# A hand-written operation list for the first three batches, put in another order

## The chip, the cores and the metric

The kernel runs on one core of one Trainium2 chip. The metric is the device time of one execution in microseconds, as the median of several runs. The times in the profile are counted from the start of its span.

## What is computed

Cosformer linear attention is followed by an MLP mixer. There are 8 batches, 8 heads, 576 positions and a head dimension of 64. Inputs and output are float32.

```python
theta = pi/2 * arange(S) / S                       # S = 576
phi(x) = concat([relu(x)*cos(theta), relu(x)*sin(theta)], -1)     # 64 -> 128 features
kv  = phi(k)^T @ v         # per batch and head: 128 x 64
z   = sum over positions of phi(k)
x   = (phi(q) @ kv) / (phi(q) @ z + 1e-6)          # heads side by side: 576 x 512 per batch
h   = relu(x^T @ w_tok1) @ w_tok2                  # mixes positions, 576 -> 256 -> 576
u   = x + h^T
out = u + relu(u @ w_ch1) @ w_ch2                  # mixes channels, 512 -> 1536 -> 512
```

## The kernel before

The 576 positions of a batch are laid on 128 partitions as four full column groups and a half one (j = 0 to 4, `J` = 4, `JA` = 5). Two batches share one tile for their half groups, `u_tail`, which is treated at the very end as if it were more batches. Raw q and k have two SBUF buffers each (even and odd batches), raw v has one. PSUM is split into two pools: `psA` with 2 buffers of two banks and `psM` with 4 buffers of one bank. A buffer is taken again only after the engine that evacuates it is done.

For a batch the steps are these; the names are the words of the operation list. `feat.b.t.j.g.f.E` computes one feature block (`f` 0 cosine, 1 sine) of q or k on engine E (L331 on ScalarE, L333 on VectorE). `cast` turns v into bfloat16 (L265). `turn` transposes q features on TensorE (L346) and `turno` evacuates them (L265); from batch 2 on `turnx` does it with a DMA on SyncE's queue (L355). `kvm` and `kvo` are kv (L362) and its copy. `num` (L391, L395) multiplies by kv, and `numo` divides on VectorE (L408, L414); `numf` and `numfo` do it for both halves of the heads (L410 to L414). `mix` is the first token product (L434), `mixo` its relu. `ux` and `ut` make the transposed u for batch 0 directly (L445, L451), `uto` copies it. `um` and `uo` make u in its normal layout (L461, L466), `tm` and `to` the tail (L489, L495). For batch 1 `ubc` casts u and `utr`, `utro` transpose it on TensorE (L481); later ones use the DMA transpose `utx` (L473). `up` is the first channel product (L513; for batch 0 the first four are split in halves of the contraction, `up.0.2.0.2` and `up.0.2.2.4`), `upo` and `upo2` its relu. `dnw` and `dnj` are the second channel product (L525), and `o` adds and stores (L537, L540).

Loads of q, k and v are `ld.b.t.g` on SyncE's queue, each of two DMAs (L144). Weights are loaded, with a conversion from float32 to bfloat16, on GpSimd's queue: `wt1` (L233), `wt2` (L239), `wu.a.n` (n of the 12 column blocks of `w_ch1` from block a, L244) and `wd.a.n` (row blocks of `w_ch2`, L249). `w2a` lays `w_tok2` out anew (L265). A last word such as `q12` in `wu.2.2.q12`, or `k02` or `wd3`, is a gate: the DMA isn't issued until that transfer has landed (q of batch 1, all heads; k of batch 0; the `wd` from block 3). `warm.0.tr.0.0.25` gives TensorE 25 transposes of zeros (L312), `warm.0.b1...` full matmuls of zeros (L322).

**What sets the order.** For batches 0, 1 and 2, and the features of batch 3, the order is the string `PLAN` (lines 17 to 57). Its words are read one after another and each issues its instructions at once (L633 to L639). Each engine takes its instructions strictly in that order, so an instruction that waits holds up all that stand behind it on the same engine, DMA issues on the SyncE and GpSimd queues among them. An engine doesn't depend on the others except by data, by buffers that come free, and by gates. The first four loads (q, k, and v in two halves of the heads, of batch 0) are issued ahead of the list (L157 to L162). 20 matmuls of zeros (L193) come first on TensorE. From batch 2's channel product on, the function `channel` runs with a table of hooks (L641 to L677); it begins at the first instruction of L590.

Of the kernel before, what the change touches and what calls it, by code (L numbers as in the profile page):

```python
# [14 lines left out]
WARM = 20  # L15
FIRST = "S"
PLAN = """
mkid feat.0.q.2.2.0.D feat.0.q.0.2.1.D feat.0.q.1.2.0.A wt1.k02 feat.0.q.3.2.0.A feat.0.q.0.2.0.D
feat.0.q.4.2.0.D feat.0.k.4.2.0.D wt2 feat.0.k.0.2.0.A feat.0.q.1.2.1.D warm.0.tr.0.0.25 turn.0.0.0 wu.4.4.k02
feat.0.k.4.2.1.D turn.0.0.1 feat.0.k.2.2.1.A feat.0.k.0.2.1.D feat.0.k.1.2.1.A feat.0.q.4.2.1.D  # L20
feat.0.k.3.2.0.A warm.0.tr.2.0.19 turn.0.2.0 turno.0.2.0.A turno.0.0.0.A cast.0.3.2.0.D feat.0.q.3.2.1.D
feat.0.k.1.2.0.D feat.0.q.2.2.1.D warm.0.tr.1.0.26 turn.0.1.0 turno.0.1.0.A cast.0.0.3.0.P feat.0.k.3.2.1.D
feat.0.k.2.2.0.D kvm.0.0 kvo.0.0.A cast.0.0.3.1.P cast.0.3.2.1.P kvm.0.1 num.0.0.0 turno.0.0.1.D numo.0.0.0
w2a.0.A warm.0.b1.0.0.4 mix.0.0.0 num.0.1.0 w2a.1.P turn.0.1.1 num.0.2.0 ld.1.q.2.v01 kvo.0.1.D num.0.0.1
turn.0.2.1 mix.0.1.0 wu.2.2.wt2 numo.0.1.0 turno.0.1.1.A mix.0.2.0 num.0.1.1 turno.0.2.1.A num.0.2.1 mix.0.3.0
numo.0.0.1 numo.0.2.0 mix.0.4.0 mixo.0.0.A wu.0.2.v01 wu.8.4 mix.0.0.1 feat.1.q.0.2.0.A numo.0.1.1 mix.0.1.1
ux.0.0 feat.1.q.0.2.1.A mix.0.2.1 mix.0.3.1 ux.0.3 numo.0.2.1 mix.0.4.1 ux.0.1 ut.0.1 mixo.0.1.D ut.0.0
uto.0.0.A ut.0.3 um.0.0 feat.1.q.4.2.0.A feat.1.q.3.2.0.D feat.1.q.1.2.1.A uto.0.1.D up.0.2.0.2 up.0.3.0.2
feat.1.q.1.2.0.D ux.0.2 ut.0.2 turn.1.0.1 uo.0.0 feat.1.q.2.2.1.A ld.1.k.2.q12 uto.0.3.D feat.1.q.3.2.1.D
uto.0.2.A up.0.0.0.2 ld.1.v.0.wu2 turn.1.0.0 feat.1.q.4.2.1.D turno.1.0.0.D feat.1.q.2.2.0.A turno.1.0.1.D  # L30
up.0.2.2.4 ld.1.v.1 turn.1.1.1 wd.9.3.k12 cast.1.4.1.0.P up.0.1.0.2 turn.1.2.0 turno.1.2.0.D turn.1.2.1 wd.0.3
up.0.0.2.4 wd.6.3.v10 up.0.1.2.4 upo2.0.0.D turno.1.1.1.A up.0.7 upo.0.7.D feat.1.k.2.2.1.A turn.1.1.0
turno.1.1.0.A feat.1.k.0.2.1.D up.0.3.2.4 up.0.10 up.0.8 tm.0 upo.0.8.A feat.1.k.4.2.0.A up.0.6 wd.3.3.v10
feat.1.k.3.2.0.D turno.1.2.1.D to.0 upo2.0.1.A ld.2.k.2.v11 up.0.11 feat.1.k.1.2.0.D upo.0.10.A
feat.1.k.0.2.0.A cast.1.0.4.0.D feat.1.k.2.2.0.D feat.1.k.1.2.1.A feat.1.k.4.2.1.D feat.1.k.3.2.1.D um.0.1
uo.0.1 cast.1.4.1.1.A upo.0.11.D up.0.4 up.0.9 upo.0.6.A upo.0.9.A kvm.1.0 ld.2.q.2.wd6 kvo.1.0.D
cast.1.0.4.1.P kvm.1.1 kvo.1.1.D upo.0.4.A ld.2.v.2.wd0 ld.3.k.2.k22 num.1.1.0 numo.1.1.0 up.0.5 upo.0.5.A
num.1.1.1 numo.1.1.1 num.1.0.0 dnw.0.0 num.1.0.1 dnw.0.1 numo.1.0.0 feat.2.k.0.2.0.A numo.1.0.1 num.1.2.1
feat.2.k.2.2.1.A dnw.0.2 feat.2.k.4.2.0.A feat.2.k.3.2.0.A feat.2.q.3.2.1.A numo.1.2.1 mix.1.0.2 ld.3.q.2.q22
mix.1.1.2 mix.1.2.2 mix.1.3.2 dnw.0.3 num.1.2.0 dnw.0.4 numo.1.2.0 feat.2.k.2.2.0.D mix.1.4.2 mixo.1.2.D.1  # L40
mixo.1.2.D.0 feat.2.q.1.2.1.A feat.2.k.4.2.1.D feat.2.q.3.2.0.A feat.2.k.3.2.1.D dnw.0.5 dnw.0.6
feat.2.q.4.2.1.D feat.2.k.1.2.1.A feat.2.q.0.2.0.D um.1.1 uo.1.1 ubc.1.1 feat.2.k.0.2.1.A dnw.0.7 um.1.0
feat.2.q.0.2.1.A tm.1 feat.2.k.1.2.0.D uo.1.0 feat.2.q.2.2.1.D cast.2.4.1.2.A dnw.0.8 feat.2.q.1.2.0.A
turnx.2.0.2 dnw.0.9 dnw.0.10 feat.2.q.4.2.0.D to.1 cast.2.0.1.2.P utr.1.1 utro.1.1.A cast.2.1.1.2.P dnw.0.11
feat.2.q.2.2.0.D turnx.2.2.2 cast.2.3.1.2.D ubc.1.0 utr.1.0 utro.1.0.A turnx.2.4.1 o.0.2 o.0.0 cast.2.2.1.2.P
o.0.3 kvm.2.2 feat.3.k.4.2.1.A feat.3.k.2.2.0.D up.1.2 upo.1.2.A up.1.3 upo.1.3.D up.1.9 up.1.8
feat.3.k.1.2.1.A o.0.1 up.1.0 upo.1.9.A feat.3.k.0.2.1.D kvo.2.2.A numf.2.1 numfo.2.1 numf.2.0 numfo.2.0
feat.3.k.4.2.0.A up.1.7 tb.1 upo.1.7.A up.1.4 upo.1.4.A numf.2.2 numfo.2.2 upo.1.0.A feat.3.q.1.2.0.A numf.2.3
up.1.6 up.1.1 mix.2.0.2 numfo.2.3 numf.2.4 numfo.2.4 feat.3.k.0.2.0.D upo.1.6.A feat.3.q.1.2.1.A mix.2.1.2
mix.2.2.2 mix.2.3.2 feat.3.q.4.2.1.A feat.3.q.0.2.1.A feat.3.k.2.2.1.D feat.3.q.0.2.0.A mix.2.4.2 mixo.2.2.A  # L50
ld.3.v.2.wd3 up.1.10 upo.1.10.D turnx.3.0.2 feat.3.q.4.2.0.A turnx.3.4.1 feat.3.q.3.2.0.A up.1.5 upo.1.1.A
upo.1.8.A feat.3.k.3.2.1.D um.2.1 uo.2.1 ubc.2.1 upo.1.5.A um.2.0 uo.2.0 up.1.11 cast.3.0.1.2.D upo.1.11.A
dnj.1.3.0 utx.2.1 dnj.1.2.0 dnj.1.1.0 feat.3.k.3.2.0.A dnj.1.2.1 cast.3.2.1.2.D feat.3.q.3.2.1.A ubc.2.0
utx.2.0 dnj.1.0.0 feat.3.q.2.2.0.D feat.3.q.2.2.1.A turnx.3.2.2 ld.4.k.2 ld.4.q.2 o.1.2 dnj.1.1.1
cast.3.3.1.2.D cast.3.1.1.2.D cast.3.4.1.2.D ld.4.v.2.k42 dnj.1.0.1 o.1.0 dnj.1.3.1 o.1.3 feat.3.k.1.2.0.A tm.2
to.2 o.1.1
"""

@with_exitstack
# [650 lines left out]
```

## Time and profile before

| what | value |
|---|---|
| median of 5 runs | 276.68 us (275.57 to 277.37) |
| the profiled execution | 276.62 us, its span 274.9 us |
| TensorE (PE) busy | 263.1 us, 96% of the span |
| VectorE (DVE) busy | 171.3 us, 62% |
| ScalarE (ACT) busy | 114.9 us, 42% |
| GpSimd (POOL) busy | 48.5 us, 18% |
| DMA | 53.37 MB, mean 194 GB/s; SyncE's queue 66.7% of the 16 engines' span, the software queue of GpSimd 9.2% |
| first instruction of L590 | 91.31 us |

The page gives busy time by engine, then the span in 40 slices of 6.9 us, in tenths. A busy TensorE is not necessarily one with useful work, since the fillers count too. The timeline of an engine gives start, length, line and tiles of each group of instructions, and in brackets how long the engine was idle ahead of it and what ended that.

### The profile page before, as it was taken

The numbers are of one execution on the slowest core, as the hardware profiler recorded it, in microseconds if no ns is written. First come the engines' busy times: TensorE is split into PE (matmuls) and PEld (weight loads), VectorE is DVE, ScalarE is ACT, GpSimd is POOL, SyncE is SP. The second block draws the span as 40 slices with busy tenths as digits, with TensorE's granted clock in tenths as the row PEclk, the third lists the DMA queues.
The fourth block names the chain that finished last, engine by engine and source line by source line (L and its number), as shares of the span: only waits on it lengthen the run. The fifth ranks groups of instructions, "written<-read, shape, count | busy, mean of one in ns | idle before, by whom it ended". The sixth has DMA issues, their size and how long they took to land.

```text
span 274.9 us, 4808 instructions
## 1 busy us (share of the span) xinstructions
PE 263.1 (96%) x1901; PEld 137.0 (50%) x1920; DVE 171.3 (62%) x341; ACT 114.9 (42%) x181; POOL 48.5 (18%) x67
## 2 busy tenths in 40 slices
PE   6779999999999999999999999999999999999994
PEld 2567646445444554455445544554455444444443
DVE  6588789498773476947683869486738634323322
ACT  2555673377781339133913392339233201301300
POOL 2282060052030032600150017001100120000000
PEclk9999999999999999999999999999999999999999
DMA  6999999999999999998999958920990052003012
GB/s 205 313 189 244 326 178 228 348 356 206 220 271 168 357 376 362 219 223 277 334 176 249 338 177 154 192 95 2 193 230 2 0 132 118 0 31 122 2 59 95
DMA packets 79079, 53.37 MB, mean 194 GB/s; under 512 B 47824, under 2 KB 76496, under 8 KB 79056
## 3 DMA queue, kind: packets, MB, share of 16 engines
q1 hardware_dynamic: 74512, 48.77, 66.7%
q0 software_dynamic: 4144, 3.77, 9.2%
q10 hardware_dynamic: 400, 0.52, 0.5%
q8 instruction: 15, 0.25, 0.4%
q14 instruction: 8, 0.07, 0.1%
HBM read 35.85 MB, written 9.44 MB: 165 GB/s over the span
## 4 chain that ended last, share of the span: by engine, by line
PE 72%; DMA 2%; DVE 1%; issue 0%
PE c_ps L590 26%; PE o_ps L607 25%; PE b L434 4%; PE u L461 4%; PE o L525 4%; PE nf L391 3%; PE kv L362 3%; DMA qpT<-qp 2%; PE c L513 1%; PE o_ps L599 1%; PE ut L489 1%; DVE x L414 1%; DVE den L411 0%; DVE u_tail L601 0%; DVE den L410 0%
## 5 line engine op out<-in xcount | busy, mean ns | idle before, releaser
L269 ACT ACTIVATE h<-c_ps 128x512 bf16<-128x512 f32 x52 | 31.0, 597 | 108.5 <-PE c_ps L590 64.3
L607 PE MATMUL o_ps<-wc,h 128*128 128x512 bf16 x317 | 71.5, 379 | 0.4
L590 PE MATMUL c_ps<-uT,wc 128*128 128x512 bf16 x288 | 70.4, 379 | 0.0
L607 PEld LDWEIGHTS <-h 128*128 128x128 bf16 x324 | 31.7, 98 | 38.2
L590 PEld LDWEIGHTS <-wc 128*128 128x128 bf16 x336 | 30.8, 98 | 32.6
L271 DVE TENSOR_SCALAR h<-c_ps 128x512 bf16<-128x512 f32 x32 | 22.0, 688 | 28.4 <-PE c_ps L590 28.4
L265 POOL CAST ub<-u 128x1024 bf16<-128x1024 f32 x14 | 15.1, 1076 | 127.5 <-DVE u L466 83.8
L610 DVE TENSOR_TENSOR u<-o_ps,u 128x512 f32<-128x512 f32 x24 | 16.5, 688 | 18.5 <-PE o_ps L607 18.5
L331 ACT ACTIVATE qp<-qt,cos_t 128x512 bf16<-128x512 f32 x31 | 21.9, 713 | 4.1 <-DMA qt<-in_q_dram 4.1
L265 POOL CAST vbf<-vt 128x512 bf16<-128x512 f32 (+3 forms) x28 | 19.7, 740 | 20.0 <-DMA vt<-in_v_dram 19.8
L513 PE MATMUL c<-uT,wc 128*128 128x512 bf16 x96 | 23.1, 379 | 0.1
L525 PE MATMUL o<-wc,h 128*128 128x512 bf16 x93 | 22.0, 379 | 0.4 <-DMA wc<-in_moe_w_ch_dram 0.2
L331 ACT ACTIVATE qp<-qt,sin_t 128x512 bf16<-128x512 f32 x31 | 21.5, 711 | 1.5 <-DMA qt<-in_q_dram 1.5
L414 DVE TENSOR_TENSOR x<-nf,den 128x512 bf16<-128x512 f32 x30 | 20.7, 691 | 1.0
L466 DVE TENSOR_TENSOR u<-u,x 128x1024 f32<-128x1024 f32 x16 | 19.4, 1218 | 1.8 <-PE u L461 1.8
L434 PE MATMUL b<-x,w 128*128 128x512 bf16 (+1 forms) x84 | 20.0, 353 | 0.4
L391 PEld LDWEIGHTS <-qpT 128*128 128x128 bf16 x320 | 14.9, 98 | 9.1 <-DMA qpT<-qp 1.2
L333 DVE TENSOR_SCALAR kp<-kt,cos_t 128x512 bf16<-128x512 f32 x30 | 17.1, 571 | 2.8 <-DMA kt<-in_k_dram 2.8
L410 DVE TENSOR_SCALAR den<-nf 128x8 f32<-128x8 f32 x30 | 5.0, 165 | 18.8 <-PE nf L391 18.8
L333 DVE TENSOR_SCALAR kp<-kt,sin_t 128x512 bf16<-128x512 f32 x31 | 16.6, 545 | 0.0
L461 PE MATMUL u<-B,w 128*128 128x512 bf16 x64 | 16.3, 379 | 0.0
L525 PEld LDWEIGHTS <-h 128*128 128x128 bf16 x96 | 9.0, 97 | 10.5 <-issue 0.5
(94 smaller groups left out, 255.5 us busy)
## 6 DMA issues: line engine op xcount, KB each, us to landing
out_dram<-u SPq DMA_DIRECT2D x32, 256.0 KB, 2.6
qt<-in_q_dram SPq DMA_DIRECT2D x8, 640.0 KB, 8.0
kt<-in_k_dram SPq DMA_DIRECT2D x8, 640.0 KB, 8.2
qt<-in_q_dram SPq DMA_DIRECT2D x8, 512.0 KB, 6.9
kt<-in_k_dram SPq DMA_DIRECT2D x8, 512.0 KB, 6.8
vt<-in_v_dram SPq DMA_DIRECT2D x6, 640.0 KB, 9.4
vt<-in_v_dram SPq DMA_DIRECT2D x6, 512.0 KB, 8.4
wc<-in_moe_w_ch_dram POOLq DMA_DIRECT2D x4, 384.0 KB, 8.5
```

Of the source, the lines that this page charges most:

```text
L265: (nc.scalar.copy if eng == "A" else ENG[eng].tensor_copy)(dst, src)
L269: nc.scalar.activation(dst, src, AF.Relu)
L331: nc.scalar.activation(dst, src, AF.Relu, scale=tab)
L333: ENG[eng].tensor_scalar(dst, src, scalar1=tab, scalar2=0.0, op0=ALU.mult, op1=ALU.max)
L391: nc.tensor.matmul(nm[:, hh * (D + 1):(hh + 1) * (D + 1)], self.qpT[:, j * H + h, :], self.kv[:, h, :D + 1], start=(not eps or hh == 0), s ...
L414: nc.vector.tensor_mul(dst, nmv[:, :, :, :D], den_b)
L434: nc.tensor.matmul(b1[:, mi], w1[:, col(self.c, j), mi * P:(mi + 1) * P], self.x[:, j, cs], start=(j == 0 and (g == 2 or mi == 0)), stop=( ...
L461: nc.tensor.matmul(ps[:, jj], w2[:, ki, 1 + 2 * g + jj, :], self.B1[:, ki, :], start=(ki == 0), stop=(ki == NT - 1))
L513: nc.tensor.matmul(ps, wc1[:, ki, mi * P:(mi + 1) * P], self.uT[:, :, ki, :], start=(ki == 0), stop=(ki == NCC - 1))
L525: nc.tensor.matmul(self.ps["o", j], self.h1[:, ki, j * P:(j + 1) * P], wc2[:, ki, :], start=(ki == 0), stop=(ki == NCH - 1))
L590: nc.tensor.matmul(c_ps, wc1[:, ki, mi * P:(mi + 1) * P], uT[:, :, ki, :], start=(ki == 0), stop=(ki == NCC - 1))
L607: nc.tensor.matmul(o_ps, h1[:, ki, j * P:(j + 1) * P], wc2[:, ki, :], start=(ki == 0), stop=(ki == NCH - 1))
```

## The change

Only the string `PLAN` differs. The two lists have the same useful operations. What is moved, taken from another engine or gated in another way, in the order of the list:

- batch 0: VectorE's first word is a k feature (it was a q feature), five q features come first on ScalarE; the transposes are in another order, with 43 + 7 + 45 fillers in place of 25 + 19 + 26, and the four full matmuls of zeros are gone;
- the first cast of v on GpSimd stands ahead of `wt1` and `wt2`, which lose their gate on k; one cast goes from GpSimd to ScalarE; `ld.1.q.2` loses its gate on v and stands near the front; `wu.4.4` goes from first to last among the `wu`;
- batch 0's transposed q are all ahead of kv; heads' half 1 is done before half 0 in kv, `num` and `mix`;
- k of batch 1 is gated on `wu8` instead of q of batch 1, the two halves of v of batch 1 on `wu4` and on nothing;
- `up.0` takes the blocks in another order (9 and 11 first); the `wd` come in the order 0, 3, 6, 9 instead of 9, 0, 6, 3;
- batch 2: q is loaded first, then k and v; `turnx.2.2.2` and `turnx.2.0.2` stand ahead of the loads of batch 3; other engines for many features, casts and evacuations.

The core of the diff:

```diff
-mkid feat.0.q.2.2.0.D feat.0.q.0.2.1.D feat.0.q.1.2.0.A wt1.k02 feat.0.q.3.2.0.A feat.0.q.0.2.0.D
-feat.0.q.4.2.0.D feat.0.k.4.2.0.D wt2 feat.0.k.0.2.0.A feat.0.q.1.2.1.D warm.0.tr.0.0.25 turn.0.0.0 wu.4.4.k02
-feat.0.k.4.2.1.D turn.0.0.1 feat.0.k.2.2.1.A feat.0.k.0.2.1.D feat.0.k.1.2.1.A feat.0.q.4.2.1.D
-feat.0.k.3.2.0.A warm.0.tr.2.0.19 turn.0.2.0 turno.0.2.0.A turno.0.0.0.A cast.0.3.2.0.D feat.0.q.3.2.1.D
-feat.0.k.1.2.0.D feat.0.q.2.2.1.D warm.0.tr.1.0.26 turn.0.1.0 turno.0.1.0.A cast.0.0.3.0.P feat.0.k.3.2.1.D
-feat.0.k.2.2.0.D kvm.0.0 kvo.0.0.A cast.0.0.3.1.P cast.0.3.2.1.P kvm.0.1 num.0.0.0 turno.0.0.1.D numo.0.0.0
-w2a.0.A warm.0.b1.0.0.4 mix.0.0.0 num.0.1.0 w2a.1.P turn.0.1.1 num.0.2.0 ld.1.q.2.v01 kvo.0.1.D num.0.0.1
-turn.0.2.1 mix.0.1.0 wu.2.2.wt2 numo.0.1.0 turno.0.1.1.A mix.0.2.0 num.0.1.1 turno.0.2.1.A num.0.2.1 mix.0.3.0
-numo.0.0.1 numo.0.2.0 mix.0.4.0 mixo.0.0.A wu.0.2.v01 wu.8.4 mix.0.0.1 feat.1.q.0.2.0.A numo.0.1.1 mix.0.1.1
...
-uto.0.2.A up.0.0.0.2 ld.1.v.0.wu2 turn.1.0.0 feat.1.q.4.2.1.D turno.1.0.0.D feat.1.q.2.2.0.A turno.1.0.1.D
-up.0.2.2.4 ld.1.v.1 turn.1.1.1 wd.9.3.k12 cast.1.4.1.0.P up.0.1.0.2 turn.1.2.0 turno.1.2.0.D turn.1.2.1 wd.0.3
...
-cast.1.0.4.1.P kvm.1.1 kvo.1.1.D upo.0.4.A ld.2.v.2.wd0 ld.3.k.2.k22 num.1.1.0 numo.1.1.0 up.0.5 upo.0.5.A
...
+feat.0.k.4.2.0.D feat.0.q.0.2.0.A feat.0.q.2.2.1.A feat.0.q.3.2.1.A feat.0.q.4.2.1.D feat.0.q.3.2.0.A
+feat.0.q.2.2.0.A mkid ld.1.q.2 warm.0.tr.1.1.43 turn.0.1.1 feat.0.k.3.2.0.A feat.0.k.4.2.1.D turn.0.1.0
+feat.0.q.1.2.1.D feat.0.q.4.2.0.A feat.0.q.1.2.0.A feat.0.k.2.2.0.D feat.0.k.1.2.1.D cast.0.0.3.0.P
+warm.0.tr.2.1.7 turn.0.2.1 turno.0.2.1.A feat.0.k.0.2.1.D cast.0.3.2.0.D feat.0.k.1.2.0.D turno.0.1.0.A
+feat.0.q.0.2.1.D warm.0.tr.0.0.45 turn.0.0.0 feat.0.k.0.2.0.D turn.0.2.0 turno.0.2.0.D feat.0.k.3.2.1.A
+feat.0.k.2.2.1.A cast.0.0.3.1.A turn.0.0.1 wt1 turno.0.1.1.D wt2 cast.0.3.2.1.P kvm.0.1 kvo.0.1.D turno.0.0.1.A
+turno.0.0.0.A kvm.0.0 kvo.0.0.A num.0.0.1 numo.0.0.1 feat.1.q.1.2.1.A num.0.2.1 numo.0.2.1 num.0.0.0 numo.0.0.0
+num.0.1.1 numo.0.1.1 mix.0.0.1 num.0.1.0 wu.2.2.q12 numo.0.1.0 wu.0.2.v00 num.0.2.0 mix.0.1.1 ux.0.3 mix.0.2.1
+mix.0.3.1 mix.0.0.0 mix.0.1.0 numo.0.2.0 mix.0.2.0 feat.1.q.3.2.0.A feat.1.q.3.2.1.D mix.0.3.0 mix.0.4.0
+feat.1.q.1.2.0.A mix.0.4.1 mixo.0.1.D wu.8.4 feat.1.q.0.2.1.A w2a.1.A feat.1.q.2.2.1.D ux.0.1 feat.1.q.4.2.1.A
+mixo.0.0.A feat.1.q.2.2.0.D w2a.0.P ut.0.3 ux.0.0 uto.0.3.D ut.0.1 uto.0.1.D tm.0 ut.0.0 um.0.1 ux.0.2 ut.0.2
+feat.1.q.0.2.0.D turn.1.0.1 uto.0.2.A to.0 turn.1.1.0 uto.0.0.D up.0.9 upo.0.9.A up.0.11 upo.0.11.A wu.4.4.q12
+turno.1.0.1.D uo.0.1 ld.1.k.2.wu8 feat.1.k.1.2.1.A um.0.0 feat.1.k.4.2.0.A feat.1.k.3.2.0.A feat.1.q.4.2.0.D
+uo.0.0 ld.1.v.1.wu4 up.0.2.0.2 up.0.3.0.2 up.0.2.2.4 turno.1.1.0.D turn.1.1.1 feat.1.k.0.2.1.D ld.1.v.0 up.0.6
+feat.1.k.4.2.1.D up.0.4 feat.1.k.2.2.0.D up.0.0.0.2 wd.0.3.k12 wd.3.3 up.0.1.0.2 turno.1.1.1.D feat.1.k.1.2.0.A
+feat.1.k.2.2.1.D up.0.0.2.4 up.0.1.2.4 upo.0.6.D turn.1.2.1 turno.1.2.1.A upo.0.4.D up.0.3.2.4 upo2.0.0.A
+up.0.10 up.0.7 upo.0.10.A wd.6.3 feat.1.k.3.2.1.D cast.1.0.4.0.D cast.1.4.1.0.D turn.1.2.0 turno.1.2.0.D
...
+kvo.1.0.D wd.9.3.v11 cast.1.0.4.1.P cast.1.4.1.1.P kvm.1.1 kvo.1.1.D dnw.0.0 num.1.2.1 numo.1.2.1 ld.2.q.2.wd3
+feat.2.q.0.2.0.A num.1.0.0 numo.1.0.0 dnw.0.1 num.1.0.1 numo.1.0.1 dnw.0.2 ld.2.k.2.wd0 feat.2.q.3.2.1.A
...
+feat.2.q.2.2.0.D ld.2.v.2 feat.2.q.4.2.1.D feat.2.k.1.2.1.A feat.2.q.3.2.0.D feat.2.q.0.2.1.D turnx.2.2.2
+uo.1.1 ubc.1.1 feat.2.k.0.2.0.A um.1.0 turnx.2.0.2 uo.1.0 dnw.0.6 feat.2.k.3.2.1.D feat.2.k.2.2.0.D
...
+feat.2.k.4.2.1.A utr.1.1 utro.1.1.D utr.1.0 utro.1.0.D cast.2.3.1.2.D ld.3.q.2.q22 cast.2.2.1.2.D
...
+cast.2.0.1.2.P kvm.2.2 kvo.2.2.A turnx.2.4.1 ld.3.k.2.wd6 o.0.3 up.1.0 upo.1.0.A up.1.9 numf.2.3 numfo.2.3
+up.1.4 upo.1.9.A numf.2.1 up.1.2 numfo.2.1 upo.1.4.A o.0.1 up.1.5 numf.2.0 upo.1.5.A upo.1.2.A numfo.2.0
+feat.3.q.3.2.0.A feat.3.q.1.2.0.A feat.3.q.2.2.0.D ld.3.v.2.v22 cast.3.4.1.2.P up.1.10 up.1.3 numf.2.2
...
```

## The prediction

> **What bounds the kernel now.** I read the page's slices first. After the first slice TensorE is busy to the end, and so is DMA up to slice 25:
>
> ```profile
> PE   6779999999999999999999999999999999999994
> ...
> DMA  6999999999999999998999958920990052003012
> ```
>
> So the kernel is TensorE's own work plus whatever time TensorE does no useful work. The change adds no useful matmul and removes none, and from slot 0 of the first `channel` call (91.3 us) on the program text is the same. The question is therefore at what time TensorE gets there. Next I read TensorE's timeline from 9 to 21 us (start, length, line; in brackets the wait before it):
>
> ```profile
> 9.16 1.56 PE L312 MATMUL tr<-ident,zero 128*128 128x128 bf16 x25
> 10.55 0.39 PE L346 MATMUL tr<-ident,qp 128*128 128x128 bf16 x4
> 12.43 0.83 PE L346 MATMUL tr<-ident,qp 128*128 128x128 bf16 x12 [1.49 <-DVE qp L333]
> ...
> 17.56 0.62 PE L346 MATMUL tr<-ident,qp 128*128 128x128 bf16 x8 [1.56 <-DVE qp L333]
> ...
> 21.21 0.38 PE L434 MATMUL b<-x,w 128*128 128x256 bf16 x2
> ```
>
> L193, L312 and L322 multiply zeros, so they are filler. TensorE waits for features. From 21 to 91 us it is dense, with a few holes. I add up the start-to-start excess of each matmul over its usual spacing (512 columns 0.216 us, 128 columns 0.056, 65 columns 0.033): the holes are 0.15 and 0.28 at 43 us, 0.37 at 50.6, 0.15 at 57.5, 0.47 at 63.3, 0.48 at 71.1 and 0.31 at 73.9, together **2.2 us**. The last two wait for transposed q (timeline, 69 to 75 us):
>
> ```profile
> 71.37 0.68 PE L391 MATMUL nf<-kv,qpT 128*128 128x65 bf16 x16 [0.32 <-DMA qpT<-qp]
> ```
>
> The features are late because VectorE is slowed. Its timeline from 11 us, and GpSimd's:
>
> ```profile
> 12.99 0.48 DVE L333 TENSOR_SCALAR qp<-qt,sin_t 128x512 bf16<-128x512 f32 x1
> 13.39 0.42 DVE L265 CAST vbf<-vt 128x512 bf16<-128x512 f32 x1
> 13.72 1.17 DVE L333 TENSOR_SCALAR qp<-qt,sin_t 128x512 bf16<-128x512 f32 x1
> 14.81 1.72 DVE L333 TENSOR_SCALAR kp<-kt,cos_t 128x512 bf16<-128x512 f32 x1
> ```
> ```profile
> 12.00 1.91 POOL L233 DMA_DIRECT2D w<-in_moe_w_tok_dram  x2 [9.98 <-DMA kt<-in_k_dram]
> 13.91 0.73 POOL L239 DMA_DIRECT2D w2r<-in_moe_w_tok_dram  x1
> 14.63 0.79 POOL L244 DMA_DIRECT2D wc<-in_moe_w_ch_dram  x1
> 15.39 2.58 POOL L265 CAST vbf<-vt 128x768 bf16<-128x768 f32 x3
> ```
>
> A VectorE feature takes 0.40 us (start to start), but the four from 13.72 take 4.45 us instead of 1.6, while GpSimd issues `w2r` and `wc` and casts. The issue of `wt1` from 12.00 slowed nothing up to 13.72.
>
> **The start, worked out.** k of batch 0 is there at 11.40 (VectorE's first kp) and q at 6.93. Both stay, since their loads are not touched.
>
> *Features.* New: VectorE's first instruction needs k, so it idles to 11.40, while ScalarE does five q features at 0.615 each from 6.94, to 10.1. VectorE then has 10 features and one cast (10 x 0.40 + 0.33 = 4.3 us), the same number as before from that time on. GpSimd's cast now stands before the weights. It waits for the first half of v (its last packet ends 1.35 us before it counts as landed, as with k; that gives 12.8), then 0.86, `wt1` 1.91, `w2r` 0.73, second cast to 17.2. I charge VectorE 0.8 for the first cast, nothing for `wt1`, 0.5 for `w2r`: it ends at 11.4 + 4.3 + 1.3 = 17.0, with the last q feature at 16.6. Before, it ended at 18.57. Bounds: nothing charged (15.7), and the 2.87 that before lost (18.6).
>
> *TensorE.* Filler 25 -> 43 (43 x 0.056 = 2.4) runs to 11.55; the first two groups of transposes are ready then. 7 and 45 fillers end at 15.55, still ahead of the features, so the 25 added fillers cost nothing; if the features came before, up to 1 us. `turn.0.0.0` 16.6, `turn.0.0.1` ends 17.7, both kv products end 19.2. ScalarE evacuates 17.9 to 19.8 (two 128x1024, 0.95 each) and then kv (0.38) at 20.2. The first normalisation on VectorE starts at 19.7 instead of 20.22, and the chain is four long (0.90) and two short (0.55) ones = 4.7, to 24.4 (before: 25.7, with a kv cast and a wait inside). `num.0.1.0` waits for that chain to free PSUM (0.9 us). One q feature, then `mixo.0.1.D` at 25.1 to 25.8, and the token product `ut` starts at 25.85. Before it started at 26.33, with one `ux` more done (4 x 0.056 = 0.22). **Lead 0.26, say 0.3 us.** With the bounds of VectorE: +1.1 and -1.3.
>
> *The weights.* `wt1`/`wt2` are issued 1.8 us later (13.8 against 12.0) and share with q of batch 1, which is no longer held back until v lands (14.53). `wt1` took 4.0 us to land on the page; with the sharing about 18.9, needed at 21.0. `wt2` about 20.3, needed by the `w2a` copies at 22. q lands at about 20.7 instead of 25.9, which fills the thin DMA stretch at 13 to 17 us; nothing needs it so early, so that is worth nothing by itself.
>
> The skill speaks on two points. In the trace VectorE lost 2.87 us beside GpSimd. The Trainium skill, "SBUF — State Buffer", section "SBUF: two separate sides", says that a two-port VectorE operation and a GpSimd one exclude each other for a whole instruction, and that weight DMAs issued from GpSimd then wait for descriptors. By it `wt1` would be stopped by VectorE's features until 17 and land after 21, a loss of 1 to 2 us; the row speaks against that part, as `wt1` was issued in 1.91 us under five back-to-back VectorE operations (12.00 to 13.91). And TensorE runs transposes alone from 8.94 to 18.0 with a granted clock of 1.00, while "TensorE: Matmul & The Clock Gate", section "Part 4: PE-mode transpose", says that these don't count as activity. By that rule the longer filler would let the clock fall; by the row it stays.
>
> **The middle.** Order in GpSimd: q lands, `wu.2`, `wu.0`, `wu.8` issued 20.7 to 23.0 (0.76 each), `w2a.0` 1.4, then `wu.4`. k of batch 1 now waits for `wu.8` instead of q. The software queue moved about 380 KB/us of f32 at 24 to 29 us (its packets), so 2.1 MB from 21.8 land at 27.7. k is issued then, 1.9 us later than before:
>
> ```profile
> 25.89 1.98 SPq L144 DMA_DIRECT2D kt<-in_k_dram  x2
> ...
> 37.73 1.30 SPq L144 DMA_DIRECT2D kt<-in_k_dram  x2
> ...
> 51.48 2.38 SPq L144 DMA_DIRECT2D kt<-in_k_dram  x2
> ```
>
> Before, k took from 25.89 to 34.65 (ScalarE's wait), 8.76 us, beside 3.6 us of weights still moving; now 2.4 us are left (`wu.4`), so about 7.6: 35.3. What is queued behind: on ScalarE and VectorE the k features stand ahead of `turno.1.1.1.D` and `upo.0.6.D`, which free PSUM for `up.0.10` (TensorE gets there at 38.7) and `up.0.7` (39.55). From landing to the first is 3 x 0.40 + 0.6 = 1.8, to the second 2.9. So k may land as late as **36.6** without a wait; 1.3 us to spare, cost nothing. kv of batch 1 (42.8) needs the last k feature, at 41.7.
>
> From 40 us on q, k, v of batch 2 are loaded one after the other behind `wd.3`, without batch 3 between them, and the DMA transposes of j 0 to 3 stand ahead of batch 3's loads. The waits for qpT (0.48 + 0.31) go, and `wd` comes in the order of use (the 0.37 goes). What is late next: the casts of v of batch 2 stand on VectorE behind five k features and two copies, done at about 62.6 where kv wants it at 62.1 (0.5, as the 0.47 before), and `up.1.4` needs the bank that `o.0.3` frees after `to.1`, 65.8 against 65.45 plus a start (0.45 new). The 0.58 of the small ones I keep. So 2.2 becomes 0.58 + 0.5 + 0.45 = 1.5: **0.7 us gained**. Below 64 us batch 3 has time: last v lands at about 79, uT of batch 2 at 88.5, wanted at 90.3.
>
> **Sum.** The profiled execution took 276.62 (span 274.85 and 1.77 around it), 0.06 below the median 276.68. 276.62 - 0.3 - 0.7 = **275.6 us**.
>
> **Rivals.**
> - *Gains eaten at the port.* VectorE loses the whole 2.87 as before. Then the start is 1.3 behind, and with 0.7 from the middle the time is 277.2. For: GpSimd is busy in the same window. Against: only two casts, not three, and no `wc` issue there.
> - *Slower: k of batch 1 too late.* `wu.8` holds it, and it passes 36.6, whereupon VectorE and ScalarE stand in their k features and TensorE stops at `up.0.10`/`up.0.7`; each us later costs one us. For: the k load of 37.73, issued while all four `wd` were queued, landed only at 51.48, 13.7 us. Issued at 27.7 that would be 41.4, a loss of 4.8, 280.4; halfway (10.6 us, 38.3) it costs 1.7, 277.3. Against: only one weight transfer is queued behind it here, not four.
> - *Nothing moves.* The lead is not there and the waits that go are replaced by others of the same size, as TensorE was dense before as well: 276.6.
>
> **How the numbers follow.** Forecast 0.50, port 0.20, k late 0.18, nothing 0.12. About 0.3% (0.83 us) can be told from no change: faster is below 275.85. Of the forecast 0.40 is below it, 0.10 not. Port: 0.13 same, 0.07 slower; k late: 0.18 slower; nothing: same. Faster 0.40, same 0.35, slower 0.25. The forecast's own range is 274.6 to 276.4; over all cases 274.2 (VectorE charged nothing, 0.8 less, and some of the kept holes gone) to 278.6 (k late by 3 us).
>
> **What would show it.** VectorE's last batch-0 k feature ends near 17.0; `ut` starts near 25.9; ScalarE's first batch-1 kp near 35.3 with no TensorE wait at 38 to 40; no wait for qpT at L391; the first L590 matmul at about 90.3 instead of 91.3. A kp after 36.6, a TensorE clock below 1.00 at 9 to 20 us, or a late `w` at L434 would make it wrong.

## The result and the profile after

| kernel | median | range | runs |
|---|---|---|---|
| before | 276.29 us | 274.56 to 277.98 | 49 |
| changed | 274.98 us | 273.81 to 277.24 | 28 |

The ratio is 0.9954 with a 95% interval of [0.9940, 0.9968]: 1.3 us faster. The profiled execution of the changed kernel took 276.57 us, near the top of its own range and hardly different from the 276.62 of the profile before. So its span says nothing on the gain; its parts do. The lines of the changed kernel stand one lower than before (L589 is the old L590).

TensorE's and the DMA's slices on the page after:

```profile
PE   6988999999999999998999999999999999999994
...
DMA  6999999999999999999999958910990062002012
```

The second and third TensorE slices, 7 and 7 before, are 9 and 8; the fourth and the one from 124 us, both 9 before, are 8. To see where the time went I cut every execution into three stretches, by starts read in the timelines: from the first k feature (k of batch 0 has landed) to the first matmul of the token product `ut` (`uT<-w,B`), from there to the first matmul of the `channel` stage (L590, now L589), and from there to the start of TensorE's last matmul. Times in us.

| profile | first k feature | k to token product | token product to `channel` | `channel` to last matmul |
|---|---|---|---|---|
| before | 11.40 | 14.93 | 64.98 | 179.33 |
| changed | 11.09 | 14.36 | 62.95 | **182.08** |

The first two stretches became 0.57 and 2.03 us shorter; the third, whose program text did not change, became 2.75 us longer. TensorE's timeline from 9 us shows the start (before it had waits of 1.49 and 1.56 there):

```profile
11.84 1.06 PE L345 MATMUL tr<-ident,qp 128*128 128x128 bf16 x16
...
16.24 1.29 PE L345 MATMUL tr<-ident,qp 128*128 128x128 bf16 x20 [0.21 <-DVE qp L332]
```

VectorE's and GpSimd's timelines in the same stretch:

```profile
13.10 1.44 DVE L332 TENSOR_SCALAR kp<-kt,sin_t 128x512 bf16<-128x512 f32 x2
14.46 0.41 DVE L264 CAST vbf<-vt 128x512 bf16<-128x512 f32 x1
14.80 0.83 DVE L332 TENSOR_SCALAR kp<-kt,cos_t 128x512 bf16<-128x512 f32 x1
```
```profile
12.81 1.05 POOL L264 CAST vbf<-vt 128x768 bf16<-128x768 f32 x1 [10.79 <-DMA vt<-in_v_dram]
13.81 1.40 POOL L232 DMA_DIRECT2D w<-in_moe_w_tok_dram  x2
```

Beside the cast the two features from 13.10 take 1.36 us to the next start instead of 0.80; the first of them runs beside the cast, the second beside the start of `wt1` and is not slowed. The waits of TensorE from 26 us to 200 us, all that the two profiles list, before and changed:

```profile
PE nf L391 <- DMA qpT<-qp: 0.3, 1, 0.3
PE kv L362 <- DVE vbf L265: 0.3, 1, 0.3
PE o L525 <- DMA wc<-in_moe_w_ch_dram: 0.2, 1, 0.2
```
```profile
PE nf L390 <- DMA qpT<-qp: 1.9, 1, 1.9
PE c_ps L589 <- DMA uT<-ub: 0.6, 1, 0.6
```

The three of before are gone. Neither of the two new ones is in the stretch that the change touched: they stand at 124.87 and 116.74, in slots of `channel`.

### The profile page after: what moved, and what is told of

It reads as the page before. It is cut to its first block, busy times and chain, and to the rows that moved or that the text cites. A ratio compares the mean times of both kernels' runs of the same rounds, so it can differ in the third digit from the quotient of the medians.

```text
span 274.8 us, 4855 instructions
## 1 busy us (share of the span) xinstructions
PE 263.1 (96%) x1923; PEld 138.0 (50%) x1941; DVE 173.1 (63%) x346; ACT 111.0 (40%) x176; POOL 47.5 (17%) x67
## 4 chain that ended last, share of the span: by engine, by line
PE 80%; DMA 10%; DVE 6%; issue 1%; SPq 0%; POOL 0%; DVEq 0%
PE c_ps L589 22%; PE o_ps L606 22%; PE c L512 8%; PE o L524 7%; PE b L433 5%; PE u L460 4%; PE kv L361 4%; DMA out_dram<-u 3%; DMA kt<-in_k_dram 3%; PE nf L390 2%; DMA qpT<-qp 2%; DMA uT<-ub 2%; DVE x L413 1%; PE tr L345 1%; DVE kp L332 1%
## 5 line engine op out<-in xcount | busy, mean ns | idle before, releaser
L589 PE MATMUL c_ps<-uT,wc 128*128 128x512 bf16 x288 | 70.4, 379 | 0.6 <-DMA uT<-ub 0.6
L606 PEld LDWEIGHTS <-h 128*128 128x128 bf16 x324 | 31.7, 98 | 38.2
L589 PEld LDWEIGHTS <-wc 128*128 128x128 bf16 x336 | 30.7, 97 | 33.4 <-issue 1.1
L264 POOL CAST ub<-u 128x1024 bf16<-128x1024 f32 x14 | 15.1, 1081 | 106.5 <-issue 62.6
L330 ACT ACTIVATE qp<-qt,cos_t 128x512 bf16<-128x512 f32 x33 | 23.1, 712 | 12.2 <-DVE den L407 7.6
L413 DVE TENSOR_TENSOR x<-nf,den 128x512 bf16<-128x512 f32 x30 | 20.7, 691 | 1.0
L332 DVE TENSOR_SCALAR kp<-kt,sin_t 128x512 bf16<-128x512 f32 x31 | 18.2, 592 | 0.2 <-DMA kt<-in_k_dram 0.2
L390 PE MATMUL nf<-kv,qpT 128*128 128x65 bf16 x240 | 12.6, 194 | 1.9 <-DMA qpT<-qp 1.9
## 6 DMA issues: line engine op xcount, KB each, us to landing
vt<-in_v_dram SPq DMA_DIRECT2D x6, 640.0 KB, 10.2
```

The lines of the kernel that those rows point to most:

```text
L264: (nc.scalar.copy if eng == "A" else ENG[eng].tensor_copy)(dst, src)
L330: nc.scalar.activation(dst, src, AF.Relu, scale=tab)
L332: ENG[eng].tensor_scalar(dst, src, scalar1=tab, scalar2=0.0, op0=ALU.mult, op1=ALU.max)
L390: nc.tensor.matmul(nm[:, hh * (D + 1):(hh + 1) * (D + 1)], self.qpT[:, j * H + h, :], self.kv[:, h, :D + 1], start=(not eps or hh == 0), s ...
L413: nc.vector.tensor_mul(dst, nmv[:, :, :, :D], den_b)
L589: nc.tensor.matmul(c_ps, wc1[:, ki, mi * P:(mi + 1) * P], uT[:, :, ki, :], start=(ki == 0), stop=(ki == NCC - 1))
```

## Experiments

Each group ran beside the kernel before on the same chip, and ratios are to it; its medians were 276.36 us (experiments 1 to 4), 275.95 (5, 6, 10, 11) and 276.15 (7 to 9, 12). A difference in us to experiment 3 is thus one between chips from experiment 5 on, where the medians of before differ by up to 0.4.

**1. The changed kernel again.**

> The changed kernel once more, unchanged. Theory (queue): TensorE reaches the first L589 matmul near 88.4 us, 2.9 us ahead of before, in every execution, and part of that is given back between 115 and 125 us, where it waits for the DMA transposes of u (batch 3) and of q (batch 4), which stand in SyncE's DMA queue behind 24 us of loads and stores without a break. The size of that wait varies with the speed of the DMAs, so the time lies 1 to 2 us below before. Rival (start): the 2.9 us are a chance of that one execution, and the lead at L589 is about the 1.3 us that the medians show, with no wait after 115 us.

274.68 us, ratio 0.9953 [0.9932, 0.9975]. Its profiled execution, 276.32 us, has the stretches 14.37, 64.15 and 181.0: again time lost behind `channel` (a wait for qpT of 1.5), and one of 0.6 at 72.14. `channel` starts at 89.23, so the lead is 2.1 us here, and not 2.9 in every execution as expected.

**2 and 3. The queue behind `channel`.** The theory: transposes of batches 3 and 4 stand in SyncE's queue behind the loads of v of batch 5, which end no earlier though TensorE is earlier. One kernel moves a transpose ahead of a load, the other lets v be loaded eight slots later.

```diff
-utx.2.1 dnj.1.0.0 utx.2.0 ld.4.q.2 dnj.1.2.0 tb.1 feat.3.k.4.2.0.A
+utx.2.1 dnj.1.0.0 utx.2.0 tb.1 ld.4.q.2 dnj.1.2.0 feat.3.k.4.2.0.A
```

> The changed kernel with one word moved: tb.1 (cast of the shared tail and its DMA transpose) stands right behind utx.2.0, ahead of the loads of batch 4, not between them. Theory (queue): in the changed kernel the DMA engines moved 25 KB in the microsecond from 92, where the queue goes from loads to this transpose and back; without that switch all of the queue up to 112 us comes about 1.5 us earlier, so the waits for uT and qpT at 115 to 125 us fall from 2.5 to about 1, and the time falls by about 0.5 to 1 us (274.2). Rival (inputs): the transposes are late because what they read is late; then the time stays (275.0).

275.0 us, ratio 0.9954 [0.9935, 0.9974]: a miss, no gain in the median over experiment 1. Its profiled execution (274.41) has the third stretch at 180.14, still 0.86 over what follows.

```diff
-            at(9, load, nxt, "v")
+            at(17, load, nxt, "v")
```

> The changed kernel with the load of v of the batch after next issued in slot 17 of channel in place of slot 9, so behind the DMA transposes of slots 10 to 16. Theory (queue): 1.18 MB at 350 KB/us leave the queue ahead of the transposes, which land 3.4 us earlier; both waits at 115 to 125 us go, and the full lead stays: 273.3 to 273.8, ratio to before about 0.990. Rival (inputs): no change, ratio 0.995.

273.51 us, ratio 0.9902 [0.9878, 0.9926], 1.2 us below experiment 1 on the same chip; third stretch 179.28. SyncE's timeline of the changed kernel, and then of this one:

```profile
98.83 3.50 SPq L143 DMA_DIRECT2D qt<-in_q_dram  x2
102.65 3.66 SPq L143 DMA_DIRECT2D vt<-in_v_dram  x2
107.08 6.93 SPq L472 DMA_TRANSPOSE uT<-ub  x2
```
```profile
98.80 2.96 SPq L143 DMA_DIRECT2D qt<-in_q_dram  x2
107.06 3.61 SPq L472 DMA_TRANSPOSE uT<-ub  x2
```

The two `uT` transposes are issued at the same time, 107.07, but with the two v loads ahead of them they take 6.93 us in the queue, without them 3.61. By the DMA packets the changed kernel moved loads and stores without a break from 93 to 112 us at about 350 KB/us, and the first 256-byte packets of the transposes only came at 112; without the v loads they came at 108.

**4. The same in the kernel before.**

> The kernel before with the same later load of v (slot 17). Theory (queue): TensorE comes 2.9 us later to the transposes there and waits for none of them after 91 us, so nothing is gained: ratio 1.000 within 0.002. Rival (the later load is better by itself, whatever the lead): ratio 0.995 as in the changed kernel.

275.88 us, ratio 0.9985 [0.9963, 1.0008], third stretch 179.28 beside 179.33: nothing to win there in the profile, and nothing clear in the time. Before, TensorE came to these transposes two to three us later, so the same queue cost it nothing.

**5 and 6. The two halves of the change alone**, v loaded in slot 17 in both. The first takes the changed list up to the first up-projection of batch 0 and finishes with the rest of the old one, the second the other way round. The seams:

```diff
 uto.0.1.D tm.0 ut.0.0 um.0.1 ux.0.2 ut.0.2 feat.1.q.0.2.0.D turn.1.0.1 uto.0.2.A to.0 turn.1.1.0 uto.0.0.D
-up.0.9 upo.0.9.A up.0.11 upo.0.11.A wu.4.4.q12
+uo.0.1 wu.4.4.k02 um.0.0 feat.1.q.4.2.0.A up.0.2.0.2 up.0.3.0.2 uo.0.0 ld.1.k.2.q12 up.0.0.0.2 ld.1.v.0.wu2
```

> The changed list up to the first up-projection of batch 0, and from there the remaining operations in the order, with the gates and on the engines of the kernel before; v of the later batches is loaded in slot 17, as in after_vlate and before_vlate, so that the queue at 115 us gives nothing back. If the lead is made in two parts (0.66 us at the start, about 2.2 us of holes in the middle), this has only the first: the token product starts near 25.5, the holes between 42 and 75 us are there again (about 2 us), the first L590 matmul starts near 90.7, and the ratio is 0.9985 - 0.66/276 = 0.996. If the start alone makes the whole gain, the ratio is 0.990; if it gives nothing, 0.9985.

275.73 us, ratio 0.9987 [0.9968, 1.0007]. The start has its 14.37 us, but the second stretch is 64.80, with a wait of 0.5 at 31 us that the seam makes. L590 starts at 89.89, with k 0.68 us earlier than in the profile before; at that landing, 90.57. The median doesn't show the start's gain: 0.9987 is what was expected if the start gives nothing (0.9985), and 0.996 lies outside the interval, a miss.

```diff
 ut.0.0 uto.0.0.A ut.0.3 um.0.0 feat.1.q.4.2.0.A feat.1.q.3.2.0.D feat.1.q.1.2.1.A uto.0.1.D
-up.0.2.0.2 up.0.3.0.2 feat.1.q.1.2.0.A ux.0.2 ut.0.2 turn.1.0.1 uo.0.0
+feat.1.q.3.2.1.D feat.1.q.1.2.0.A feat.1.q.2.2.1.D feat.1.q.4.2.1.A feat.1.q.2.2.0.D uto.0.3.D tm.0 um.0.1
```

> The list of the kernel before up to the first up-projection of batch 0, and the rest as changed, v of the later batches in slot 17 again. By the two parts this has only the second: the token product starts near 26.3, no hole of over 0.2 us stands between 42 and 75, the first matmul of the channel stage starts near 89.1, and the ratio is 0.9985 - 2.2/276 = 0.9905. If the early start is what takes the holes away (k and v of batches 1 and 2 get ahead by it), the holes are back and the ratio is 0.9985.

276.77 us, ratio 1.0035 [1.0014, 1.0056]: a miss. The u product waits 2.4 us at 28 us, because VectorE has q features of batch 1 ahead of the tail's sum (L495) that frees the PSUM buffer, and with the old start q lands only at 27.2.

**7. The same with q loaded early.**

```diff
-feat.0.q.4.2.0.D feat.0.k.4.2.0.D wt2
+feat.0.q.4.2.0.D ld.1.q.2 feat.0.k.4.2.0.D wt2
...
-num.0.2.0 ld.1.q.2.v01 kvo.0.1.D
+num.0.2.0 kvo.0.1.D
```

> startB_restA with one edit: the load of q of batch 1 is issued early and ungated, as in the changed list, instead of waiting for v. If the 2.4 us wait of the u product at 28 us (and the 1.4 us of half clock behind it) came only from q landing at 27.2 us, both go, the way from the first token product to the channel stage takes 62.7 to 63.0 us instead of 65.0 to 65.8, and the ratio is 0.988 to 0.991. If the middle gains nothing without the earlier start, the ratio stays near 0.9985.

276.6 us, ratio 1.0021 [1.0002, 1.0041]: a miss again. Two of TensorE's waits:

```profile
PE u L461 <- DVE u_tail L495: 1.3, 1, 1.3
PE c L513 <- DVE h L271: 0.7, 1, 0.7
```

The first is half gone. But `w2r`, issued at 13.01 while q is still being loaded, lands only at 20.8; the first of the three `wu` that follow is gated on it, and all three stand behind its copy on GpSimd. They are issued from 22.2 (from 17.8 in the changed kernel, where the first is gated on q), k of batch 1, gated on `wu8`, at 31.7, and its features start at 38.15. So the new middle is not a gain by itself. In these runs it pays only behind the new start, with its order of q and weights.

**8. The early q alone**, taken out of experiment 3, with `wu.2` on its old gate.

```diff
-feat.0.q.2.2.0.A mkid ld.1.q.2 warm.0.tr.1.1.43
+feat.0.q.2.2.0.A mkid ld.1.q.2.v01 warm.0.tr.1.1.43
...
-num.0.1.1 numo.0.1.1 mix.0.0.1 num.0.1.0 wu.2.2.q12
+num.0.1.1 numo.0.1.1 mix.0.0.1 num.0.1.0 wu.2.2.wt2
```

> after_vlate with the load of q of batch 1 gated on v again and wu.2 on wt2, as before. By the prediction's step (the early q is worth nothing by itself) the time stays at 273.5. If the new order of the middle lives on the early q, its features stand on VectorE ahead of the copies that free PSUM, the u product waits about 2.4 us at 28 us, half clock follows, and the time is 276 to 277.5.

277.51 us, ratio 1.0055 [1.0033, 1.0077], 4.0 us above experiment 3. The time is as expected, but TensorE stops earlier than at the u product. GpSimd's timeline, then TensorE's:

```profile
22.99 2.25 POOL L243 DMA_DIRECT2D wc<-in_moe_w_ch_dram  x3 [6.23 <-DMA w2r<-in_moe_w_tok_dram]
25.22 1.59 POOL L264 COPY w<-w2r 128x640 bf16<-128x640 bf16 x1
```
```profile
26.94 0.59 PE L450 MATMUL uT<-w,B 128*128 128x512 bf16 x2 [2.33 <-POOL w L264]
```

`w2r` lands at 22.99 instead of about 21, the copy of it stands behind three `wu` issues, and TensorE waits for the copy. The old gate of `wu.2` can hardly be the cause: q itself lands only then (its first feature on ScalarE starts at 22.97), and the gate on q would have held the `wu` as long. k is late too: its features start at 39.70.

**9. k of batch 1 one weight later**, again out of experiment 3.

```diff
-turno.1.0.1.D uo.0.1 ld.1.k.2.wu8
+turno.1.0.1.D uo.0.1 ld.1.k.2.wu4
```

> after_vlate with k of batch 1 gated on the last up-weight (wu.4) instead of the one before it, so that its load is issued at about 30.8 instead of 28 us and lands near 37.2. If the prediction's threshold of 36.6 holds, TensorE stops at the up-projections of 38 to 40 us for 0.6 to 2.5 us, and the time is 274.1 to 276. If there was more to spare than 1.3 us, nothing moves: 273.5.

275.32 us (274.29 to 277.58), ratio 0.9984 [0.9952, 1.0016]: 1.8 us above experiment 3, and a wide spread. The profiled execution (274.44) is near the bottom of that range. Its k features start at 35.93, and the waits of TensorE include

```profile
PE kv L361 <- DVE h L270: 0.4, 1, 0.4
...
PE c L512 <- DVE h L270: 0.2, 1, 0.2
```

with start-to-start excesses of 0.38 at 38.8, 0.18 at 42.4 and 0.57 at 43.4.

**10 and 11. The loads of batch 3 and the q transposes of batch 2.** First the old order of the queue in the list of experiment 3, then the new order in the list of before (v in slot 17).

```diff
-feat.2.q.0.2.1.D turnx.2.2.2
+feat.2.q.0.2.1.D ld.3.q.2.q22 ld.3.k.2.wd6 turnx.2.2.2
```

> after_vlate with the loads of q and k of batch 3 put back ahead of the DMA transposes of q of batch 2 on SyncE's queue. If it is the order in this queue that makes the holes at 71 to 74 us, L390 waits for qpT again, for 0.8 us (as before) up to 3 us, and the time is 0.8 to 3 us above after_vlate's 273.5. If the holes went because other things got ahead, nothing moves: within 0.4 us of 273.5.

279.46 us, ratio 1.0122 [1.0093, 1.0151], 5.95 us above experiment 3, more than the 3 expected. Its waits, and the windows behind the wait (stretch, its length, PE, PEld, DVE, ACT and POOL busy, then the granted clock):

```profile
PE nf L390 <- DMA qpT<-qp: 4.1, 2, 3.8
```
```profile
63.00:68.00 5.00, 1.21 (x13) 0.56 (x12) 1.12 (x2) 1.19 (x2) 0.00 (x0) 1.00 1.10 170
68.00:70.00 2.00, 1.66 (x14) 0.76 (x12) 1.18 (x4) 0.60 (x1) 0.00 (x0) 0.74 1.18 264
70.00:72.00 2.00, 2.00 (x6) 0.73 (x5) 1.54 (x4) 0.00 (x0) 0.00 (x0) 0.50 0.54 217
```

The waits are 4.1 us; most of the rest is TensorE at half its clock from 69.0 to 72.4, behind them, which costs half of these 3.4 us.

```diff
-kvo.1.1.D upo.0.4.A ld.2.v.2.wd0 ld.3.k.2.k22 num.1.1.0
+kvo.1.1.D upo.0.4.A ld.2.v.2.wd0 num.1.1.0
...
-numo.1.2.1 mix.1.0.2 ld.3.q.2.q22
+numo.1.2.1 mix.1.0.2
...
-utr.1.0 utro.1.0.A turnx.2.4.1 o.0.2
+utr.1.0 utro.1.0.A turnx.2.4.1 ld.3.k.2 ld.3.q.2 o.0.2
```

> before_vlate with the loads of q and k of batch 3 put behind the DMA transposes of q of batch 2: one move of the change made alone. If the order in the queue makes the holes at 71 to 74 us, L391's waits for qpT (0.48 and 0.31) go and the ratio is 0.9985 - 0.8/276 = 0.9957; if not, it stays at 0.9985. A loss (over 1.0) would say that batch 3 needs these loads early.

285.32 us, ratio 1.0340 [1.0310, 1.0370]: a loss of 9 us, the number of neither theory. TensorE's one wait between 60 and 95 us, and VectorE's timeline:

```profile
PE c L513 <- DVE h L271: 8.9, 1, 8.9
```
```profile
73.75 0.49 DVE L333 TENSOR_SCALAR kp<-kt,cos_t 128x512 bf16<-128x512 f32 x1 [9.37 <-DMA kt<-in_k_dram]
74.16 0.69 DVE L271 TENSOR_SCALAR h<-c 128x512 bf16<-128x512 f32 x1
```

A feature of batch 3 stands in the old list ahead of the copy that frees PSUM. The later load holds that feature, the feature holds the copy. At 68.8, still in the wait, the clock falls to half as well, until 79.1. So in the old list the new queue order is a loss; with the later places of these features, as in the changed list, it is none.

**12. The best version.** Experiment 3 with `tb.1` moved as in experiment 2, and the q load of batch 3 behind the last q transposes of batch 2. This last edit was for a wait in experiment 3, whose VectorE and TensorE timelines show it:

```profile
70.62 0.49 DVE L332 TENSOR_SCALAR qp<-qt,cos_t 128x512 bf16<-128x512 f32 x1 [2.01 <-DMA qpT<-qp]
```
```profile
72.29 0.42 PE L390 MATMUL nf<-kv,qpT 128*128 128x65 bf16 x8 [0.72 <-DVE x L413]
```

A feature of batch 3 can't be written before the transposes have read the tile, and behind it on VectorE stands the division that frees PSUM.

```diff
-cast.2.3.1.2.D ld.3.q.2.q22 cast.2.2.1.2.D
+cast.2.3.1.2.D cast.2.2.1.2.D
...
-turnx.2.4.1 ld.3.k.2.wd6 o.0.3
+turnx.2.4.1 ld.3.q.2.q22 ld.3.k.2.wd6 o.0.3
```

> after_vlate with the transposes of uT's tail of batch 1 moved ahead of the q load of batch 4, and the q load of batch 3 behind the last q transposes of batch 2, against the 0.88 us wait at 71 us. If that wait stands in most executions: 272.7 (ratio 0.987). If it stands only in the slowest ones, as after_vlate's own times say (five of six are 0.7 to 1.0 us under its profiled 274.41), the time is 273.3 to 273.5 (ratio 0.990).

272.92 us (272.66 to 273.30), ratio 0.9890 [0.9862, 0.9918], the lowest median here, between the two values expected; its interval overlaps that of experiment 3. Stretches 14.36, 62.94 and 179.29, and no wait of TensorE between 26 and 135 us.

The stretches of the other profiles:

| profile | first k feature | k to token product | token product to `channel` | `channel` to last matmul | features of batch 1's k |
|---|---|---|---|---|---|
| 1 changed, again | 10.71 | 14.37 | 64.15 | 181.00 | 35.10 |
| 2 tail transposes earlier | 10.84 | 14.37 | 62.94 | 180.14 | 33.66 |
| 3 changed, v late | 11.20 | 14.36 | 63.82 | 179.28 | 34.57 |
| 4 before, v late | 10.59 | 14.93 | 65.83 | 179.28 | 34.52 |
| 5 new start | 10.72 | 14.37 | 64.80 | 179.28 | 34.67 |
| 6 new middle | 10.67 | 14.92 | 67.24 | 179.29 | 37.77 |
| 7 new middle, early q | 10.50 | 15.52 | 65.59 | 179.28 | 38.15 |
| 8 late q | 10.91 | 16.03 | 66.49 | 179.28 | 39.70 |
| 9 k later | 10.86 | 14.36 | 64.17 | 179.28 | 35.93 |
| 10 old queue order | 10.81 | 14.37 | 69.03 | 179.28 | 35.02 |
| 11 before, new queue order | 10.56 | 14.92 | 75.30 | 179.28 | 34.26 |
| 12 best | 10.48 | 14.36 | 62.94 | 179.29 | 34.02 |

## Why the prediction was right, and which steps were not

The number held: 275.6 predicted, 274.98 measured, faster. As a gain it is 1.0 against 1.3 us, since the five runs that the sum started from lay 0.4 above the median of all 49. But part of this is luck: the sum was off in two places in opposite directions, a gain in the middle that was put too low and a loss behind `channel` that wasn't in it.

**The start, 0.3 us: right.** From k to the token product it is 14.92 or 14.93 us in all four profiles with the old start and the late q (before, 4, 6, 11), and 14.36 or 14.37 in all that keep the changed start with its early q. That is 0.57 us; less the one `ux` (0.22), 0.35. The 0.88 that the two profiled executions show (26.33 to 25.45) is 0.31 of k landing earlier; k lands anywhere between 10.48 and 11.40. The last VectorE feature ended at 16.92 (17.0 predicted), 5.83 us behind k where the sum had 5.6. The first cast cost VectorE 0.56 (0.8 charged), and the last three features, beside `w2r` and the second cast, lost 0.84 (0.5 charged). `wt1` was issued in 1.40 us beside running features and landed at 19.28. So the rule of the Trainium skill, "SBUF — State Buffer", section "SBUF: two separate sides", by which `wt1` would have been stopped until 17, did not show here; the page ties it to VectorE's two-port mode, and no run here shows whether these features use it. TensorE's granted clock is 1.00 in the changed kernel from 9.4 to 17.6 us, where it runs fillers and transposes alone, against the Trainium skill, "TensorE: Matmul & The Clock Gate", section "Part 4: PE-mode transpose".

**"That is worth nothing by itself" (the early q): failed.** Without the early load the list of experiment 3 is 4.0 us slower (experiment 8). It loses already at the start, with 16.03 us from k to the token product in place of 14.36, as `w2r` lands late beside q, and k of batch 1 comes late behind it. The new middle behind the old start stops for 2.4 us (experiment 6). The step asked who needs q early; it should have asked as well what shares the DMA engines with q when it is loaded later.

**k of batch 1 at 35.3, 36.6 allowed: close on the landing, too generous on the limit.** It was there at 33.66 to 35.10 in the profiles of the changed gate, and TensorE didn't wait at 38 to 40. The landing came close partly by luck: q landed at 17.5, not 20.7, so the `wu` were issued 3 us earlier than in the sum, and yet k could be issued only at 28.22 (27.7 in the sum). And a k of 35.93 costs 1.1 us (experiment 9), one of 35.10 already opens a hole of about 0.2 at 42.6 (experiment 1). So the limit lay near 35, not at 36.6, and the rival "k too late" was a near one.

**The middle, 0.7 us: mis-sized.** All 2.2 us of holes of before went: 62.95 is the stretch without waits (62.94 in experiments 2 and 12). I had kept 1.5. None of the three parts came: v of batch 2 was cast by 61.1 where I had put 62.6, and kv at 60.81 ran through; `up.1.4` stood behind no wait; the small holes at 43 went. In other executions a hole is there (0.88 in experiment 3; 1.2 in all in experiment 1), so the gain is 0.8 to 2.0 on the profile before, whose stretch varies too (65.83 in experiment 4, with the same list up to there).

**"From slot 0 of the first `channel` call on the program text is the same": true, but I took it to mean that the time is the same. This was the failed step.** The third stretch grew from 179.33 to 182.08. TensorE comes earlier to transposes that SyncE's queue carries behind the loads of batch 5, so the lead runs into a limit that before cost nothing. Experiments 3 and 4 show it: with v later the stretch is 179.28 and 1.2 us more is gained (experiment 3 against 1), while the kernel before gains nothing clear (0.9985, its interval takes in 1). How much the median execution of the changed kernel gives back is not seen in a profile, since both profiled ones lie near the top of the range; 276.57 - 2.80 = 273.77 would be this one without it, so about 1.2 us at the median of 274.98, an estimate that fits the 1.2 of experiment 3. Its fastest run is 273.81.

Open: why the give-back differs so much between executions of one kernel (2.80 in one, 1.72 in the other), and why experiment 2, with 0.86, isn't faster in the median. What the first half alone is worth isn't settled either, as each half spoils something at its seam.

## What to carry to other kernels

A lead won early is kept only as far as the next limit: where the text behind an edit is unchanged, look at which queue is just in time there, and take the lead off its slack. In lists of strictly ordered engines single moves are not additive; one move of this change alone lost 9 us here, because a load that is moved later holds a feature, and the feature holds a copy that frees PSUM. Compare stretches between events of the trace, not spans: they repeat to 0.05 us where nothing waits, while whole executions differ by 3 us.

## What the runs showed of the hardware

- **A wait of over two us can cost TensorE its clock as well.** After waits of 2.33, 2.44 and 3.79 us (experiments 8, 6, 10) the granted clock falls to 0.50 for 3.4 us (0.66 in the mean of 26 to 31 us in experiment 8), and for 10.2 us at the 8.9 us wait of experiment 11; after 1.3 (experiment 7) and 1.87 us (changed kernel, at 123 us) it stays 1.00. The Trainium skill, "TensorE: Matmul & The Clock Gate", section "Why this matters for your kernels", warns of gaps beyond about 3 us; here 2.33 was enough. It also counts where a wait falls. In all four runs the drop comes a whole multiple of 3.41 us after the clock's first rise to 1.00 (20.48, 23.90, 61.44 and 61.44 us). In the 3.41 us just ahead of these drops TensorE was idle for 2.33, 2.44, 2.12 and 2.81 us; in no other such piece of any run here that ran at 1.00, up to 250 us, was it idle for more than 1.74, and there the clock stayed. The 1.87 us of the changed kernel lie across two pieces, with at most 1.12 in one.
- **DMA transposes wait in SyncE's queue for the loads ahead of them** (the two `uT` of experiment 3: 6.93 us with two loads of v ahead, 3.61 without). Around the transposes single microseconds are nearly empty: 25 KB at 92, 42 at 113 and 17 at 116 us in the changed kernel, beside some 350 KB in a full one. In experiment 2, where the tail's transpose stands ahead of the loads, the microsecond at 92 is full and one at 86 has 33 KB. What empties them isn't shown.
